# A two-block decode attention kernel on one Trainium2 core: transposing K as fp32 pairs, five of eight heads on VectorE in place of four, and moving copies to ScalarE

## The chip, the cores and the metric

The kernel runs on one core of one Trainium2 chip. The metric is the device time of one execution in microseconds (us); medians are over several executions. A verdict of "faster" or "slower" means more than 2%.

Words used below: PE is TensorE, DVE is VectorE, ACT is ScalarE, POOL is GpSimd, SP is SyncE, which issues all the DMA transfers here. "Landing" is the moment when a part of a transfer reports to its semaphore.

## The reference

Two independent attention blocks, A and B, each with one query token per sequence, 8 sequences, 32 heads, 4096 cached keys and values per head, head size 128, all in bf16. The outputs are set side by side.

```python
def _A_ref(x, k_cache, v_cache, wq, wo):          # _B_ref is the same
    q = (x @ wq).reshape(B, 1, 32, 128).transpose(0, 2, 1, 3)
    scores = einsum("bhqd,bhkd->bhqk", q, k_cache) * 128 ** -0.5
    p = softmax(scores)
    o = einsum("bhqk,bhkd->bhqd", p, v_cache)
    return o.transpose(0, 2, 1, 3).reshape(B, 1, 32 * 128) @ wo
# out = concatenate([A, B], axis=-1)
```

There are 2 blocks x 32 heads x 8 sequences = 512 pairs of (sequence, head); each needs 1 MB of K and 1 MB of V, read once. That is 1.07 GB of 1.11 GB in all, and the data queue fills 96.9% of the DMA engines' time in the profile below, so the loads are the limit to look at first. What can be tuned is what stands in their way.

## The kernel before

A "group" is one head with its 8 sequences; a "K head" is the 1 MB of K of one sequence and head. There are 64 groups. K has 6 slots in SBUF (`Kb`), V has 8 (`Vb`), each of 1 MB. One queue, on SP, issues every load in program order; a K load waits until the head six places earlier has been released.

```python
DL = cfg.get("DL", 10); NK = cfg.get("NK", 6); NV = cfg.get("NV", 8)
DVB = list(cfg.get("DVB", (1, 3, 5, 7)))          # sequences whose scores VectorE computes
PEB = [b for b in range(NB) if b not in DVB]      # the others go through PE
...
def k_released(m):
    if is_pe(m):
        return (pe_tq, NQ * (e_idx(m) + 1))       # all four quarters transposed
    return (dve_qk, v_idx(m) + 1)                 # VectorE's dot products done
...
w = [k_released(n - NK)] if n >= NK else []
    return sp.dma_start(Kb[:, n % NK, :], Ks[blk][b, h].rearrange("(p j) d -> p (j d)", p=128))
```

The scores of a head on the PE path: 32 transposes of 128x128 into PSUM, four evictions to SBUF by ACT, then 32 matmuls with one column of q.

```python
for jj in range(8):                                # emit_T, one quarter of a head
    j = q * 8 + jj
    ins = pe.transpose(dst[:, jj * 128:(jj + 1) * 128], Kb[:, kslot, j * 128:(j + 1) * 128], ident[:])
```

The scores of a head on the VectorE path: 32 dot products over 128 elements, of one position of K per partition with a copy of q that PE has spread over all partitions. In the trace each is two instructions, the product with its sum (8,192 of them, 284 ns in the mean) and the read of the accumulator (8,192, 80 ns), so a head is 64 VectorE instructions.

```python
for jj in range(8):                                # dqk_item, one quarter of a head
    j = 8 * k + jj
    ins = d.tensor_tensor_reduce(junk[:, j, :], Kb[:, kslot, j * 128:(j + 1) * 128], q_rep[:, par, r, :],
                                 1.0, 0.0, ALU.mult, ALU.add, S2[:, par, r, j:j + 1])
```

The softmax then runs per group (maximum on DVE and POOL, exponentials on ACT), PE multiplies with V ten heads later, and the output projection follows. DVE also copies PSUM results that later steps need (`q_rep`, `Dg_sb`, and some small ones) and clears one PSUM bank per group.

## Time and profile before

The median was 2789.04 us of 5 runs (2785.41 to 2790.54).

| engine | busy, us | share of the span |
|---|---|---|
| data queue on the DMA engines | | 96.9% |
| PE | 2051.4 | 74% |
| DVE | 1941.2 | 70% |
| ACT | 714.4 | 26% |

The page of the kernel before, its parts 1 to 4: the busy time of each engine with its number of instructions; the DMA engines' mean busy share and their rate in 40 equal slices of the span; the DMA queues with packets, MB and share of the 16 engines' time; and the chain of work that ended last, by engine ("SPq" and the like are the parts of an engine that issue its instructions; "issue" is time in which an engine waited for nothing that the profile shows).

```profile
PE 2051.4 (74%) x22304; PEld 1352.4 (49%) x22304; DVE 1941.2 (70%) x16975; ACT 714.4 (26%) x2049; POOL 51.8 (2%) x136
...
DMA  9999999989999899998999989999899998999996
GB/s 390 419 419 414 396 420 419 409 357 407 419 417 400 353 416 419 417 398 347 416 419 416 406 339 420 419 414 403 348 419 420 416 409 345 418 419 412 402 396 265
...
q1 hardware_dynamic: 165056, 1107.43, 96.9%
q8 instruction: 179, 2.93, 0.4%
q14 instruction: 174, 1.42, 0.1%
...
DMA 66%; PE 17%; DVE 13%; SPq 2%; issue 1%; ACT 0%; POOL 0%; DVEq 0%; POOLq 0%; ACTq 0%
```

The loads pace the kernel, and PE and DVE wait for them. But the rate is not the 419 GB/s of the best slices throughout: it dips to about 350 at regular places and averages 397. Two lines are the queues of kind "instruction". They carry the engines' own program, as two runs below show: 4,096 more VectorE instructions take q14 from 174 packets to 205 (e1_waits), 8,192 more PE instructions take q8 from 179 to 211 (e9_pewaits). Beside the data queue they are nothing (2.93 and 1.42 MB, 0.4% and 0.1% of the time).

Groups of instructions of the kernel before (line, engine, operation, out<-in, shapes, count | busy us, mean ns of one | idle time before them and what ended it):

```profile
L373 DVE CUSTOM_DVE_ANT_0 junk<-Kb,q_rep 128x128 bf16<-128x128 bf16 x8192 | 1772.4, 284 | 426.4 <-DMA Kb<-in_B_k_cache_dram 200.8
L214 PE MATMUL ps<-ident,Kb 128*128 128x128 bf16 x8192 | 704.1, 265 | 714.5 <-DMA Kb<-in_B_k_cache_dram 361.4
...
L373 DVE DVE_READ_ACCUMULATOR2_ANT S<- 128x1 f32 x8192 | 655.8, 80 | 0.0
```

Both score paths spend hundreds of us idle in front of K loads. One dip, around the load of the second piece of `wq`, in the windows view of the kernel before (stretch in us; stretch's length, then busy time and count of PE, PE's weight loads, DVE, ACT, POOL; granted clock; DMA share; GB/s):

```profile
610.00:620.00 10.00, 10.00 (x136) 6.66 (x135) 7.48 (x67) 2.05 (x4) 0.00 (x0) 1.00 0.92 361
620.00:630.00 10.00, 7.26 (x82) 5.20 (x80) 8.03 (x69) 2.29 (x4) 0.00 (x0) 0.83 0.19 53
630.00:640.00 10.00, 1.57 (x8) 0.48 (x5) 7.06 (x65) 0.00 (x0) 0.36 (x1) 0.84 1.01 416
```

This looks as if the loads stood still for 8 us because nobody had released a slot. The landing records of the trace tell it otherwise. Each of the 1,096 large transfers leaves 16 landings in the trace, which are read here as one from each of the 16 DMA engines that the page counts; no record names the engine of a landing. Sorted by time, for the transfers around this dip (us from the start of the span):

```
transfer   first landing   last landing   later than the last landing before it
V            608.51          627.12          3.42
K            610.99          629.58          2.46
V            613.48          632.09          2.51
wq (2 MB)    618.82          639.10          7.01
K            632.12          641.60          2.50
```

Fifteen of the 16 landings of this batch were in by 621 us, and no first landing came again until 632 us; the last ones went on without a hole. Over the whole trace, the 15 earlier landings of a K or V transfer come 13 to 15 us before the last one in the mean: one landing alone is late, and the author's reading, which no record shows, is that it is always the same engine's. Nothing shows a pause in the late landings: they follow each other at a median of 2.49 us per 1 MB, with 142 gaps that are longer by more than 0.5 us (over 2.5 us for K and V, 7.0 for `wq`, 0.65 for `wo`), nearly all of them by 0.9 to 1.0 us. Of these 142 gaps, 138 stand beside an 8,192-byte packet of q14.

The built program has 17,797 VectorE instructions. PE's count gives an estimate of the size of one: 22,048 matmuls of two instructions each plus 1,296 others are 45,392 in the built program, and q8 carried 2.93 MB in 179 packets of 16,384 bytes, so 64 to 65 bytes each. By that estimate a packet of 8,192 bytes is 128 instructions (e1_waits added 4,096 and 31 packets, 132 a packet), and VectorE's program is 139 such blocks, close to the number of the gaps. (q14 carries more than that: 174 packets here, 204 against 170 blocks in the changed kernel, 61 against 27 in e5_few below, so some 35 more in each. The built program has 4,002 instructions on ACT, POOL and SP, which would be 31 blocks. About 30 packets of q14 stand beside no gap, so by this count it is VectorE's part of q14 that goes with the gaps, not q14 as such.)

### The profile page before, as it was taken

The numbers are of one execution on the slowest core, as the hardware profiler recorded it, in microseconds if no ns is written. First come the engines' busy times: TensorE is split into PE (matmuls) and PEld (weight loads), VectorE is DVE, ScalarE is ACT, GpSimd is POOL, SyncE is SP. The second block draws the span as 40 slices with busy tenths as digits, with TensorE's granted clock in tenths as the row PEclk, the third lists the DMA queues.
The fourth block names the chain that finished last, engine by engine and source line by source line (L and its number), as shares of the span: only waits on it lengthen the run. The fifth ranks groups of instructions, "written<-read, shape, count | busy, mean of one in ns | idle before, by whom it ended". The sixth has DMA issues, their size and how long they took to land.

```text
span 2787.1 us, 68208 instructions
## 1 busy us (share of the span) xinstructions
PE 2051.4 (74%) x22304; PEld 1352.4 (49%) x22304; DVE 1941.2 (70%) x16975; ACT 714.4 (26%) x2049; POOL 51.8 (2%) x136
## 2 busy tenths in 40 slices
PE   6777777776877767777777676776777777777777
PEld 4444454454554544445445454454544444444444
DVE  7777666776767767676676766767767677577775
ACT  3222222222222222222222222222222222222221
POOL 0000000000000000000000000000000000000000
PEclk8898888988889888988898888988888989798889
DMA  9999999989999899998999989999899998999996
GB/s 390 419 419 414 396 420 419 409 357 407 419 417 400 353 416 419 417 398 347 416 419 416 406 339 420 419 414 403 348 419 420 416 409 345 418 419 412 402 396 265
DMA packets 165409, 1111.78 MB, mean 399 GB/s; under 512 B 17569, under 2 KB 17569, under 8 KB 33985
## 3 DMA queue, kind: packets, MB, share of 16 engines
q1 hardware_dynamic: 165056, 1107.43, 96.9%
q8 instruction: 179, 2.93, 0.4%
q14 instruction: 174, 1.42, 0.1%
HBM read 1107.33 MB, written 0.03 MB: 397 GB/s over the span
## 4 chain that ended last, share of the span: by engine, by line
DMA 66%; PE 17%; DVE 13%; SPq 2%; issue 1%; ACT 0%; POOL 0%; DVEq 0%; POOLq 0%; ACTq 0%
DMA Kb<-in_B_k_cache_dram 34%; DMA Kb<-in_A_k_cache_dram 32%; DVE junk L373 12%; PE ps L240 7%; PE ps L214 6%; SPq L629 2%; PE ps L227 1%; PE ps L285 1%; SPq L624 1%; DMA Vb<-in_B_v_cache_dram 1%; DVE S L373 1%; PE ps L263 0%; PE ps L294 0%; DVE acc L417 0%; DVE Dg_sb L578 0%
## 5 line engine op out<-in xcount | busy, mean ns | idle before, releaser
L373 DVE CUSTOM_DVE_ANT_0 junk<-Kb,q_rep 128x128 bf16<-128x128 bf16 x8192 | 1772.4, 284 | 426.4 <-DMA Kb<-in_B_k_cache_dram 200.8
L214 PE MATMUL ps<-ident,Kb 128*128 128x128 bf16 x8192 | 704.1, 265 | 714.5 <-DMA Kb<-in_B_k_cache_dram 361.4
L330 ACT COPY KT<-ps 128x512 f32<-128x512 f32 x1024 | 564.2, 592 | 2019.6 <-PE ps L214 2017.3
L240 PE MATMUL ps<-Vb,Ppad 128*32 128x512 bf16 x4096 | 1038.4, 399 | 3.4 <-issue 1.8
L214 PEld LDWEIGHTS ps<-ident,Kb 128*128 128x128 bf16 x8192 | 651.0, 122 | 791.8 <-DMA Kb<-in_B_k_cache_dram 400.7
L373 DVE DVE_READ_ACCUMULATOR2_ANT S<- 128x1 f32 x8192 | 655.8, 80 | 0.0
L240 PEld LDWEIGHTS ps<-Vb,Ppad 128*32 128x32 bf16 x4096 | 370.4, 100 | 459.3 <-issue 106.9
L227 PEld LDWEIGHTS ps<-q_all,KT 128*128 128x128 bf16 x8192 | 222.8, 96 | 82.4 <-issue 80.2
L227 PE MATMUL ps<-q_all,KT 128*128 128x1 bf16 x8192 | 244.9, 164 | 0.4
L404 DVE TENSOR_TENSOR oT<-ps,rL 128x8 bf16<-128x8 f32 x64 | 10.7, 167 | 242.1 <-PE ps L285 242.1
L349 ACT ACTIVATE Ppad<-S,negM 128x32 bf16<-128x32 f32 x256 | 82.0, 320 | 0.0
L349 ACT ACTIVATE Ppad<-ps,negM 128x32 bf16<-128x32 f32 x256 | 72.9, 285 | 29.9 <-DVE negM L567 29.9
L285 PEld LDWEIGHTS ps<-Sel,Dg_sb 32*128 32x128 f32 x512 | 62.6, 188 | 28.4 <-issue 27.1
L285 PE MATMUL ps<-Sel,Dg_sb 32*128 32x8 f32 x512 | 68.2, 255 | 3.6 <-DVE q_all L385 2.9
L604 POOL PARTITION_ALL_REDUCE M_sb<-m_sb x64 | 23.4, 366 | 2440.2 <-DVE m_sb L537 2440.2
L417 DVE TENSOR_TENSOR acc<-ps,acc 128x64 f32<-128x64 f32 x62 | 13.9, 225 | 69.3 <-PE ps L294 69.0
L349 ACT ACTIVATION_READ_ACCUMULATOR Ppad<-ps,negM 128x1 f32 x256 | 52.0, 203 | 0.0
L578 DVE COPY Dg_sb<-ps 32x512 f32<-32x512 f32 x64 | 43.1, 674 | 12.3 <-PE ps L240 12.3
L349 ACT ACTIVATION_READ_ACCUMULATOR Ppad<-S,negM 128x1 f32 x256 | 51.2, 200 | 0.0
L395 DVE CAST q_rep<-ps 128x512 bf16<-128x512 f32 x64 | 43.7, 682 | 6.5 <-PE ps L274 5.0
L544 DVE MEMSET ps<- 32x512 f32 x64 | 31.0, 485 | 5.9
L567 DVE TENSOR_SCALAR negM<-M_sb 128x8 f32<-128x8 f32 x64 | 11.0, 172 | 31.5 <-POOL M_sb L604 31.5
(29 smaller groups left out, 196.3 us busy)
## 6 DMA issues: line engine op xcount, KB each, us to landing
Kb<-in_A_k_cache_dram SPq DMA_DIRECT2D x256, 1024.0 KB, 25.1
Vb<-in_A_v_cache_dram SPq DMA_DIRECT2D x256, 1024.0 KB, 26.5
Kb<-in_B_k_cache_dram SPq DMA_DIRECT2D x256, 1024.0 KB, 25.4
Vb<-in_B_v_cache_dram SPq DMA_DIRECT2D x256, 1024.0 KB, 26.5
wq_sb<-in_A_wq_dram SPq DMA_DIRECT2D x4, 2048.0 KB, 31.3
wo_sb<-in_A_wo_dram SPq DMA_DIRECT2D x32, 256.0 KB, 26.5
wq_sb<-in_B_wq_dram SPq DMA_DIRECT2D x4, 2048.0 KB, 32.7
wo_sb<-in_B_wo_dram SPq DMA_DIRECT2D x32, 256.0 KB, 26.7
```

The costliest lines, as they stand in the source:

```text
L214: ins = pe.transpose(dst[:, jj * 128:(jj + 1) * 128], Kb[:, kslot, j * 128:(j + 1) * 128], ident[:])
L227: ins = pe.matmul(S[:, c:c + 1], lhsT=KT[:, e_idx(n) % 2, j * 128:(j + 1) * 128], rhs=q_all[:, G, b:b + 1], start=True, stop=True)
L240: ins = pe.matmul(Dg(par), lhsT=Ppad[:, par, b, c].rearrange("p a m -> p (a m)"), rhs=Vb[:, vslot, c * 512:(c + 1) * 512], start=False, st ...
L285: ins = pe.matmul(Mp_f[:, 0:NB], lhsT=Dg_sb[0:32, par, jj * 128:(jj + 1) * 128], rhs=Sel[0:32, jj, :], start=(jj == 0), stop=(jj == 3))
L330: return a.copy(dst, src)
L349: return a.activation(Ppad[:, par, b, :, b, :], src.rearrange("p (c m) -> p c m", m=4), ACTF.Exp, bias=negM[:, par, b:b + 1], scale=SCALE, ...
L373: ins = d.tensor_tensor_reduce(junk[:, j, :], Kb[:, kslot, j * 128:(j + 1) * 128], q_rep[:, par, r, :], 1.0, 0.0, ALU.mult, ALU.add, S2[:, ...
L395: return d.tensor_copy(q_rep[:, G % 2, :, :].rearrange("p r d -> p (r d)"), Mp_f[:, 0:NDV * 128])
L544: return d.memset(Dg(G % 2), 0.0)
L578: return d.tensor_copy(Dg_sb[:, G % 2, :], Dg(G % 2))
L624: return sp.dma_start(Kb[:, n % NK, :], Ks[blk][b, h].rearrange("(p j) d -> p (j d)", p=128))
L629: return sp.dma_start(Vb[:, n % NV, :], Vs[blk][b, h].rearrange("(p j) d -> p (j d)", p=128))
```

## The change

The intent: relieve PE, ACT and the copies, and use VectorE's 30% of free time. K is read as fp32 elements, each a pair of bf16 values, so a head needs 16 transposes in place of 32; the matmuls then take every second column of the result with a q vector that has been permuted and masked (`Qe`). Five of eight sequences go to VectorE in place of four. The copies of `q_rep`, `q_all`, `xT`, `Dg_sb` and `o_sb` go from VectorE to ACT, and the clearing of the PSUM bank is replaced by the start flag of the first matmul. Cut to its core:

```diff
-    DVB = list(cfg.get("DVB", (1, 3, 5, 7)))
+    DVB = list(cfg.get("DVB", (1, 2, 4, 5, 7)))
...
+                if T1:
+                    dst = ktp_f(bank)
+                    kf = Kb[:, kslot, :].bitcast(f32)
+                    for tt in range(4):
+                        t = q * 4 + tt
+                        ins = pe.transpose(dst[:, tt * 128:(tt + 1) * 128], kf[:, t * 128:(t + 1) * 128], ident_f[:])
+                    return ins
...
+                    for tt in range(4):
+                        t = q * 4 + tt
+                        c = b * NJ + 2 * t
+                        for e in range(2):
+                            ins = pe.matmul(S[:, c:c + 2], lhsT=ktb[:, t * 256 + e:(t + 1) * 256:2],
+                                            rhs=Qe[:, G % 2, pe_rank[b], e, :], start=(e == 0), stop=(e == 1))
...
-                                    start=False, stop=(c == NCH - 1), skip_group_check=True)
+                                    start=(b == 0 and c == 0), stop=(b == NB - 1 and c == NCH - 1), skip_group_check=True)
...
+        COPY_ENG = cfg.get("COPY_ENG", "act")
+        def cp(eng, dst, src):
+            return eng.copy(dst, src) if COPY_ENG == "act" else eng.tensor_copy(dst, src)
...
-                    add("dve", f"QSC{s}", w, [(dve_mp, 1)], f)
+                    add(which, f"QSC{s}", w, [(dve_mp, 1)], f)
...
-                return d.memset(Dg(G % 2), 0.0)
-            add("dve", f"ZERO{G}", w, [(dve_z, 1)], f)
```

(Left out: the set-up of the permutation and mask tiles, the small matmul pair per group that makes `Qe`, and the reordering of the maxima.)

## The prediction

> **What bounds the kernel now.** The page's slices show the 16 DMA engines 90% busy or more nearly throughout; the queue table gives the data queue 96.9%, the chain of waits gives DMA 66%. PE is busy 74%, VectorE 70%: no compute engine is the limit.
>
> More exactly, I think one DMA engine is. Every transfer leaves 16 landing records in the trace. From about 30 us on, 15 of them come together and one comes some 13 us later. The last landings follow each other without a hole: median 2.49 us per 1 MB K or V head, except for 142 gaps longer by about 0.97 us (138 us in all). Of those, 138 fall beside an 8192-byte packet of the instruction queue q14 (174 on the page). 8192 bytes would be 128 instructions: the 17,797 VectorE instructions of the built program make 139 such blocks. So my reading: the DMA engine that fetches VectorE's instructions loses about 1 us per fetch and is the slowest. The other 15 wait for it through the K and V slots (the stretch 620 to 630 us at 53 GB/s is such a wait). It never runs dry: the next transfer was issued a median of 28 us, never under 8.7 us after the start, before it finished the last.
>
> [...]
>
> **What the change does.**
> - PE: 16 transposes per K head for 32, 3 of 8 K heads for 4. Matmuls in the program fall from 22,048 to 15,072. PE waits about 710 us for K before (waits view): off the critical path.
> - ACT: loses a quarter of its evictions (564 us before), gains copies (about 0.68 us each). Off the path.
> - VectorE: loses two copies and a memset per group (43.7 + 43.1 + 31.0 us), gains 64 heads of 32 dot products at 0.2125 us (start to start in the timeline), 6.8 us each: +435 us. Busy goes from 1941 to about 2265 us, some 80%. Its waits for PE and PoolE (about 400 us before) still fit; two neighbouring VectorE heads lag the arrivals by some 3 us, inside the 28 us of slack.
> - VectorE instructions: 17,797 to 21,760, so 139 to 170 fetches: +31 at about 0.97 us on the slowest DMA engine.
> - HBM bytes are unchanged.
>
> **Sum.** Nothing removed is on the critical path; about 30 us of DMA work is added to it: 2789 + 30 = 2819 us, range 2806 to 2834. Faster by over 2%: 0.03; within 2%: 0.90; slower by over 2%: 0.07.
>
> **What would show it.** q14 packets up by about 30, q8 packets down; about 172 gaps of 1 us in the last landings; still exactly one late landing of 16; median spacing 2.49 us; VectorE busy 2200 to 2330 us; PE busy well down; mean about 395 GB/s; DMA still over 95% busy and leading the chain.
>
> **What would make it wrong.** Waits between VectorE, ACT and PE (ACT's copies stand in line behind evictions and exponentials) could exceed the slack, so that VectorE paces: over 2845 us. Or the fetches are a coincidence and the time stays at 2789; or PE's fetches, which fall, cost the slowest engine too, and the time falls by tens of us. The end could grow by a few us, two of the last three heads being VectorE's.

## The result, and the profile after

The changed kernel took 2827.93 us (median of 8 runs, 2823.57 to 2829.9) against 2789.87 us of before (15 runs). The ratio is 1.013, 95% interval 1.0115 to 1.0145: slower by 1.3%, within the 2% band. A ratio here is the mean time of one kernel's fast runs over that of the other's in the same rounds, so it is not quite the ratio of the medians.

The page of the changed kernel, the same parts:

```profile
PE 1916.8 (68%) x15328; PEld 1227.2 (43%) x15328; DVE 2272.4 (80%) x20935; ACT 685.6 (24%) x1997; POOL 52.1 (2%) x138
...
DMA  8999999999999899998999989999899998999996
GB/s 357 420 419 418 377 419 418 391 371 389 420 402 395 362 397 419 405 400 348 417 415 407 397 338 420 419 405 399 334 419 416 401 394 344 420 418 398 402 386 260
...
q1 hardware_dynamic: 165056, 1107.43, 96.4%
q8 instruction: 124, 2.03, 0.3%
q14 instruction: 204, 1.67, 0.1%
...
DMA 52%; DVE 31%; PE 13%; SPq 2%; issue 1%; ACT 0%; DVEq 0%; POOL 0%; POOLq 0%
```

The data queue moved the same 1107.43 MB. q14 went from 174 packets to 204, q8 from 179 to 124. PE lost 135 us of busy time, VectorE gained 331. Groups of the changed kernel:

```profile
L409 DVE CUSTOM_DVE_ANT_0 junk<-Kb,q_rep 128x128 bf16<-128x128 bf16 x10240 | 2212.0, 288 | 322.4 <-DMA Kb<-in_B_k_cache_dram 154.7
...
L229 PE MATMUL ps<-ident_f,Kb 128*128 128x128 f32 x3072 | 620.7, 386 | 505.1 <-DMA Kb<-in_B_k_cache_dram 267.0
...
L409 DVE DVE_READ_ACCUMULATOR2_ANT S<- 128x1 f32 x10240 | 849.9, 83 | 0.1
```

Both paths still wait for K loads for hundreds of us, so neither paces the kernel, although VectorE is 80% busy. The dip of the same `wq` load, in the windows view of the changed kernel:

```profile
620.00:630.00 10.00, 9.98 (x77) 6.49 (x78) 6.49 (x62) 2.35 (x4) 0.00 (x0) 0.74 0.97 382
630.00:640.00 10.00, 4.46 (x25) 3.50 (x23) 9.83 (x93) 2.03 (x4) 0.00 (x0) 0.77 0.13 40
640.00:650.00 10.00, 6.13 (x53) 2.96 (x51) 8.22 (x75) 1.17 (x2) 0.37 (x1) 0.84 0.95 364
```

The dip has only moved. The landing records of both profiled runs, counted the same way, and how many us later than in the run before a given transfer had landed (in the order of their last landings, numbered from 0):

```
                                     before   changed
gaps longer by more than 0.5 us         142       170
of these beside a q14 packet            138       164
median spacing of last landings, us    2.49      2.49
last landing of transfer 40, us      114.09    119.41  (+5.3)
last landing of transfer 400, us    1025.16   1041.80  (+16.6)
last landing of transfer 1095, us   2779.01   2815.85  (+36.8)
end of the span, us                  2787.1    2824.4  (+37.3)
```

The waits view has new entries (engine and line, what it waited for: us in total, times, longest us). Before:

```profile
DVE oT L404 <- PE ps L285: 242.1, 64, 5.9
...
DVE acc L417 <- PE ps L294: 69.0, 59, 2.8
```

In the changed kernel:

```profile
PE ps L312 <- DVE Qe L453: 326.3, 64, 18.2
...
DVE acc L476 <- PE ps L332: 158.3, 62, 3.9
...
DVE oT L463 <- PE ps L323: 14.0, 2, 13.2
```

PE now waits for VectorE once per group, and VectorE for PE at another place. Whether such waits matter is decided by the loads: about 5 us are lost in the first 40 us, and the rest comes evenly along the run, as 28 further gaps of 1 us would. A run below tells it too: with the VectorE heads in another order (e8_order), PE's wait for `Qe` is 54 us, and DVE's two waits are back near those of the kernel before (`acc` 64 us, `oT` 244 us), and the time stays that of the changed kernel.

### The profile page after: what moved, and what is told of

It is laid out like the page before. It is cut to its first block, busy times and chain, and to the rows that moved or that the text cites. A ratio compares the mean times of both kernels' runs of the same rounds, so it can differ in the third digit from the quotient of the medians.

```text
span 2824.4 us, 58099 instructions
## 1 busy us (share of the span) xinstructions
PE 1916.8 (68%) x15328; PEld 1227.2 (43%) x15328; DVE 2272.4 (80%) x20935; ACT 685.6 (24%) x1997; POOL 52.1 (2%) x138
## 3 DMA queue, kind: packets, MB, share of 16 engines
q1 hardware_dynamic: 165056, 1107.43, 96.4%
## 4 chain that ended last, share of the span: by engine, by line
DMA 52%; DVE 31%; PE 13%; SPq 2%; issue 1%; ACT 0%; DVEq 0%; POOL 0%; POOLq 0%
DVE junk L409 29%; DMA Kb<-in_B_k_cache_dram 27%; DMA Kb<-in_A_k_cache_dram 24%; PE ps L229 7%; PE ps L269 5%; DVE S L409 1%; SPq L715 1%; SPq L720 1%; DMA Vb<-in_B_v_cache_dram 1%; PE ps L332 1%; DVE Qe L453 0%; PE ps L312 0%; DVE acc L476 0%; PE ps L250 0%; ACT q_rep L417 0%
## 5 line engine op out<-in xcount | busy, mean ns | idle before, releaser
L409 DVE CUSTOM_DVE_ANT_0 junk<-Kb,q_rep 128x128 bf16<-128x128 bf16 x10240 | 2212.0, 288 | 322.4 <-DMA Kb<-in_B_k_cache_dram 154.7
L229 PE MATMUL ps<-ident_f,Kb 128*128 128x128 f32 x3072 | 620.7, 386 | 505.1 <-DMA Kb<-in_B_k_cache_dram 267.0
L409 DVE DVE_READ_ACCUMULATOR2_ANT S<- 128x1 f32 x10240 | 849.9, 83 | 0.1
L229 PEld LDWEIGHTS ps<-ident_f,Kb 128*128 128x128 f32 x3072 | 554.7, 205 | 546.1 <-DMA Kb<-in_B_k_cache_dram 285.4
L366 ACT COPY KT<-ps 128x512 f32<-128x512 f32 x768 | 436.5, 590 | 1188.2 <-PE ps L229 1187.2
L312 PE MATMUL ps<-ident,q_all 128*128 128x128 bf16 x320 | 54.4, 293 | 375.4 <-DVE Qe L453 326.3
L417 ACT CAST q_rep<-ps 128x512 bf16<-128x512 f32 (+1 forms) x128 | 54.5, 426 | 782.9 <-PE ps L312 782.9
L250 PEld LDWEIGHTS ps<-Qe,KT 128*128 128x128 bf16 x6144 | 167.6, 97 | 54.3 <-issue 53.5
L250 PE MATMUL ps<-Qe,KT 128*128 128x2 bf16 x6144 | 182.7, 163 | 0.3
L476 DVE TENSOR_TENSOR acc<-ps,acc 128x64 f32<-128x64 f32 x62 | 13.9, 225 | 158.3 <-PE ps L332 158.3
L586 ACT COPY Dg_sb<-ps 32x512 f32<-32x512 f32 x64 | 36.8, 575 | 103.9 <-PE ps L269 103.9
```

Of the source, the lines that this page charges most:

```text
L229: ins = pe.transpose(dst[:, tt * 128:(tt + 1) * 128], kf[:, t * 128:(t + 1) * 128], ident_f[:])
L250: ins = pe.matmul(S[:, c:c + 2], lhsT=ktb[:, t * 256 + e:(t + 1) * 256:2], rhs=Qe[:, G % 2, pe_rank[b], e, :], start=(e == 0), stop=(e == 1))
L312: ins = pe.matmul(Mp_f[:, r * 128:(r + 1) * 128], lhsT=q_all[:, G, b:b + 1].broadcast_to([128, 128]), rhs=ident[:], start=True, stop=True)
L366: return a.copy(dst, src)
L417: return eng.copy(dst, src) if COPY_ENG == "act" else eng.tensor_copy(dst, src)
L586: return a.copy(Dg_sb[:, G % 2, :], Dg(G % 2))
```

## The experiments

Every run gave correct results. "Blocks" are VectorE instructions of the built program over 128; "gaps" are counted as above, in the profiled run.

| run | VectorE instructions (blocks) | q14 | q8 | VectorE busy, us | gaps | median, us | ratio to before (95%) |
|---|---|---|---|---|---|---|---|
| before | 17,797 (139) | 174 | 179 | 1941 | 142 | 2789 | |
| changed | 21,760 (170) | 204 | 124 | 2272 | 170 | 2828 | 1.013 (1.0115 to 1.0145) |
| e1_waits | 21,893 (171) | 205 | 179 | 1949 | 171 | 2824.1 | 1.0115 (1.0093 to 1.0136) |
| e2_busy | 18,053 (141) | 175 | 179 | 2389 | 142 | 2797.3 | 1.0021 (1.0002 to 1.0039) |
| e3_pairs | 17,600 (138) | 174 | 148 | 1842 | 138 | 2786.7 | 0.9985 (0.9964 to 1.0006) |
| e4_rebal | 22,024 (172) | 202 | 147 | 2365 | 178 | 2835.5 | 1.0158 (1.0136 to 1.018) |
| e5_few | 3,461 (27) | 61 | 179 | 2057 | 29 | 2688.5 | 0.9645 (0.9628 to 0.9663) |
| e6_few_pairs | 3,264 (26) | 62 | 148 | 1958 | 22 | 2682.9 | 0.9621 (0.9607 to 0.9635) |
| e7_few_after | 3,840 (30) | 64 | 124 | 2421 | 31 | 2687.6 | 0.9636 (0.962 to 0.9653) |
| e8_order | 21,760 (170) | 204 | 124 | 2283 | 169 | 2825.7 | 1.0133 (1.0118 to 1.0148) |
| e9_pewaits | 17,797 (139) | 173 | 211 | 1945 | 138 | 2791.1 | 1.0007 (0.9991 to 1.0023) |
| e10_after | 21,760 (170) | 204 | 124 | 2272 | 169 | 2824.8 | 1.013 (1.0116 to 1.0145) |
| e11_order | 21,760 (170) | 204 | 124 | 2282 | 172 | 2825.4 | 1.0133 (1.012 to 1.0146) |
| e12_best | 2,560 (20) | 54 | 124 | 2282 | 23 | 2684.9 | 0.9631 (0.9615 to 0.9647) |

(For e3_pairs and e4_rebal the expectations below have 17,539 and 21,890 instructions; these are the numbers of the programs as built.)

The theory on trial, the author's reading of the 142 gaps and the q14 packets beside them: one DMA engine serves VectorE's instruction fetches, loses about 1 us of loading per fetch, and is the slowest; the kernel's time is that engine's time. What the runs can show of it is landings, packets and time, not the engine. The rivals: VectorE's work itself slows the loads or the releases; the copies on ACT or the pairs make new waits; the rate of the memory is simply a ceiling.

### Instructions without work: e1_waits

The kernel before, with waits on a semaphore that has long been up. In the built program its 8,192 waits are 4,096 instructions more (17,797 to 21,893).

```diff
             def f(d, par=par, r=r, kslot=kslot, k=k):
                 ins = None
+                for _ in range(8):
+                    d.wait_ge(s_id, 1)
```

> The kernel before with 4,096 more VectorE instructions that do nothing: waits on a semaphore that is already up (17,797 to 21,893 instructions, 139 to 171 blocks of 128). VectorE's work is unchanged. Fetch theory: 32 more fetches at about 0.97 us each, +31 us, 2820 us (2813 to 2828), about 30 more q14 packets and about 174 gaps of 1 us. Rival (the change costs VectorE work, or waits between engines): VectorE's busy time is unchanged and so is the time, 2785 to 2795 us.

Measured: ratio 1.0115, which on 2789 us is +32 us (26 to 38). The page of e1_waits, parts 1 and 3:

```profile
PE 2069.0 (73%) x22304; PEld 1360.8 (48%) x22304; DVE 1949.4 (69%) x16975; ACT 716.5 (25%) x2049; POOL 52.1 (2%) x136
...
q8 instruction: 179, 2.93, 0.4%
q14 instruction: 205, 1.68, 0.1%
```

VectorE did the same 16,975 counted instructions for about the same busy time; the added ones do no work and are not even counted as busy. Only q14 grew, by 31 packets, and the gaps grew by 29. Nearly the whole loss of the change came back with nothing but instructions to fetch.

### Work without instructions: e2_busy

One reduction more per VectorE head, into a tile that nobody reads.

```diff
+                if k == 0:
+                    d.tensor_reduce(extra[:], Kb[:, kslot, 0:1664], AX.X, ALU.max)
```

> The kernel before with one extra VectorE reduction over 1,664 elements of each of its 256 K heads: about 1.7 us each, +435 us of VectorE work, as much as the change adds, but only 256 more instructions (2 blocks). Fetch theory: +2 us, plus up to 3 us at the start, 2788 to 2797 us. Rival (VectorE's work or its SBUF reads slow the loads): about +37 us as in the change, 2820 to 2830 us.

Measured: ratio 1.0021, +6 us (1 to 11). The median of 2797.28 us is just over the top of what was expected. The page of e2_busy:

```profile
PE 2059.4 (74%) x22304; PEld 1352.7 (48%) x22304; DVE 2388.9 (85%) x17231; ACT 716.3 (26%) x2049; POOL 50.8 (2%) x136
...
q14 instruction: 175, 1.43, 0.1%
```

VectorE was busier (85%) than in the changed kernel (80%), and the loss was a sixth of the change's. So VectorE's work is not the main cause; but some us do come with it. The two added blocks would make about 2 (an estimate, from 0.97 us a gap), though the gaps of the trace did not grow. In the trace 3 us of it are at the end: from the last landing to the end of the span it takes 11.3 us, 8.1 before.

### The change in parts: e3_pairs and e4_rebal

e3_pairs is the changed kernel with the old split:

```diff
-    DVB = list(cfg.get("DVB", (1, 2, 4, 5, 7)))
+    DVB = list(cfg.get("DVB", (1, 3, 5, 7)))
```

> The changed kernel with the split put back to four heads each; K transposed in pairs and the copies on ACT stay. VectorE has 17,539 instructions (137 blocks against 139), PE 18,080 matmuls against 22,048. Fetch theory: -2 us, 2783 to 2792 us, q14 packets within 5 of before. Rival (the copies on ACT or the pair set-up cause the loss by waits): most of the +37 us stays. Second rival (fewer PE fetches help): clearly under 2780 us.

Measured: 2786.65 us, ratio 0.9985 (0.9964 to 1.0006), the same time as before. Its page, parts 1 and 3:

```profile
PE 2065.3 (74%) x18336; PEld 1337.2 (48%) x18336; DVE 1841.7 (66%) x16839; ACT 791.8 (28%) x2189; POOL 52.4 (2%) x138
...
q8 instruction: 148, 2.42, 0.4%
q14 instruction: 174, 1.43, 0.1%
```

Pairs, copies on ACT and the missing memset neither cost nor gain anything that shows: they work on engines that wait (PE 648 us and VectorE 490 us for K loads in the waits view of this run, ACT 1492 us for PE's transposes).

e4_rebal is the changed kernel with the new split, but without pairs and without the copies on ACT (the start flag in place of the memset stays):

```diff
-    T1 = cfg.get("T1", True)
+    T1 = cfg.get("T1", False)
-        COPY_ENG = cfg.get("COPY_ENG", "act")
+        COPY_ENG = cfg.get("COPY_ENG", "dve")
```

> The changed kernel with the split of five VectorE heads kept, but K transposed in bf16 as before and the copies on VectorE. VectorE has 21,890 instructions (171 blocks, 32 more than before). Fetch theory: +31 us, and about +5 us at the start as in the changed kernel: 2818 to 2834 us. Rival (pairs or copies cause the loss): back near 2789 us.

Measured: 2835.54 us, ratio 1.0158 (1.0136 to 1.018). The loss is all in the rebalance, and it is a little over the top of the range. Its trace has 178 gaps and was already 8 us behind before at transfer 40. With the copies back on it VectorE is 83% busy. The other two parts of the change may hide a part of what the rebalance costs (1.0158 against 1.013), but the two intervals overlap.

### Fewer instructions for the same heads: e5_few, e6_few_pairs, e7_few_after

If fetches are the price, 64 instructions per head are the fault and not the head. The head's quarter becomes one multiplication of 1,024 elements and one sum over it:

```diff
-                for jj in range(8):
-                    j = 8 * k + jj
-                    ins = d.tensor_tensor_reduce(junk[:, j, :], Kb[:, kslot, j * 128:(j + 1) * 128], q_rep[:, par, r, :],
-                                                 1.0, 0.0, ALU.mult, ALU.add, S2[:, par, r, j:j + 1])
+                js = slice(8 * k, 8 * k + 8)
+                d.tensor_tensor(junk[:, js, :], Kb[:, kslot, 1024 * k:1024 * (k + 1)].rearrange("p (j d) -> p j d", d=128),
+                                q_rep[:, par, r, :].unsqueeze(1).broadcast_to([128, 8, 128]), ALU.mult).then_inc(dve_tt, 1)
+                d.wait_ge(dve_tt, 4 * vi + k + 1)
+                ins = d.tensor_reduce(S2[:, par, r, js], junk[:, js, :], AX.X, ALU.add)
```

(The products are now rounded to bf16 before they are summed.)

> The kernel before with VectorE's 64 instructions per K head (32 dot products, each with a read of its accumulator) replaced by 8: four multiplications of 1,024 elements and four sums. VectorE's instructions fall from 17,797 to 3,461, 139 blocks to 27, for the same head count. Fetch theory: 112 fetches fewer on the slowest DMA engine, so that engine's own need falls to about 2789 - 112 x 0.97 = 2680 us; PE's 179 fetches on q8 then show whether another engine is next (estimate: at most 0.77 us each, or that engine would have been the slowest already, so at most 2790). So 2675 to 2765 us, clearly faster, if VectorE keeps pace; by an estimate from the 128-wide reductions a head takes 7 to 9.5 us, 31 to 41 us of a 42 us group, so VectorE may become the limit. Rival (the DMA rate of about 399 GB/s is a ceiling of memory, fetches do not matter): 2785 to 2795 us.

Measured: 2688.48 us, ratio 0.9645. The page of e5_few, parts 1, 2, 3 and 5:

```profile
PE 2012.1 (75%) x22304; PEld 1318.0 (49%) x22304; DVE 2057.1 (76%) x2639; ACT 714.4 (27%) x2049; POOL 53.8 (2%) x136
...
DMA  9999999999999999999999999999999999999996
GB/s 388 420 420 420 417 420 420 420 418 416 420 420 420 405 417 419 420 420 396 419 420 420 420 403 396 419 420 420 396 420 420 420 420 396 421 420 420 420 420 279
...
q1 hardware_dynamic: 165056, 1107.43, 99.4%
q8 instruction: 179, 2.93, 0.4%
q14 instruction: 61, 0.50, 0.0%
...
L376 DVE TENSOR_REDUCE S<-junk 128x8 f32<-128x1024 bf16 x1024 | 1249.4, 1220 | 35.4
```

VectorE is busier than before (2057 against 1941 us), and the kernel is 3.6% faster. The dips are nearly gone: the slices stand at 420 GB/s, the data queue fills 99.4%. So the dips were in the main not the cost of the `wq` load or of slots released too late by the arithmetic; they went with VectorE's instructions (139 blocks to 27, 142 gaps to 29). That 15 engines waited there for the sixteenth is the author's reading. (The 14th, 19th, 24th, 29th and 34th slices, 339 to 353 GB/s before, still read 396 to 405.) 29 gaps are left, most of them by 1.2 to 1.7 us and about 120 us apart; 26 of them stand beside a q8 packet, 5 beside one of q14. PE's fetches come every 15 us (2688 over 179), so a gap is at every eighth.

e6_few_pairs is the same loop in the changed kernel with the old split.

> The same 8 instructions per VectorE head, on the changed kernel's code with the split of four and four: pair transposes, copies on ACT. PE matmuls 18,080 against 22,048, so about 148 fetches on q8 for 179; VectorE 3,264 instructions (26 blocks). Fetch theory: if PE's fetch engine is the next slowest, this run is faster than the one with 179 (31 fetches at the cost that that run shows, up to 20 us); if PE's fetches are free, the two agree within 5 us. Rival: no difference to before.

Measured: 2682.93 us, ratio 0.9621. It is 5.5 us below e5_few in the median, at the edge of what the expectation set apart, with 22 gaps in place of 29, now about 143 us apart: PE's fetches come every 18 us there (2683 over 148), so it is the eighth again. The intervals of the two ratios just overlap.

e7_few_after is the same loop in the changed kernel, five heads on VectorE.

> The changed kernel (five VectorE heads, pairs, copies on ACT) with 8 VectorE instructions per head: 3,840 instructions (30 blocks) for 21,760, q8 about 124 fetches. Fetch theory: the whole loss of the change disappears and more, 2665 to 2750 us, if five heads fit in VectorE's 42 us per group (7 us a head or less); if a head takes over 8.4 us VectorE paces at 5 heads, 2800 us or more, with VectorE over 95% busy. Rival (the change loses because of VectorE's share of the heads): at least 2815 us even with VectorE below 90%.

Measured: 2687.62 us, ratio 0.9636, with VectorE 90% busy. Its page, parts 1 and 3:

```profile
PE 1878.6 (70%) x15328; PEld 1198.7 (45%) x15328; DVE 2421.3 (90%) x3015; ACT 679.8 (25%) x1997; POOL 54.6 (2%) x138
...
q14 instruction: 64, 0.52, 0.0%
```

The rival that blames VectorE's share of the heads needed 2815 us. With few instructions the split makes no difference that shows. Of this run's 31 gaps, 27 stand beside q14 packets again: VectorE's 30 blocks are more than an eighth of PE's 124 packets (15.5); that this is why was not shown.

### Whose fetches: e9_pewaits

The kernel before with 8,192 empty instructions on PE, twice the bytes of e1_waits.

```diff
             def f(pe):
                 dst = ktp_bf(bank)
                 ins = None
+                for _ in range(16):
+                    pe.wait_ge(s_id, 1)
```

> The kernel before with 8,192 more PE instructions that do nothing (waits on a semaphore already up): 32 more 16 KiB blocks on q8, 512 KiB more of fetched instructions, twice the bytes that the 4,096 VectorE waits added on q14. Theory (only fetches that land on the slowest DMA engine cost[...]): no change, 2785 to 2793 us. Rival (any instruction fetch takes its time from the loads): +31 us or more, 2820 us.

Measured: 2791.11 us, ratio 1.0007 (0.9991 to 1.0023): no change. Part 3 of its page:

```profile
q8 instruction: 211, 3.46, 0.5%
q14 instruction: 173, 1.42, 0.1%
```

32 more packets of 16,384 bytes cost nothing, where 31 of 8,192 bytes on q14 had cost 32 us. So it is not the bytes fetched. That it is the DMA engine on which they fall is the author's reading (the gaps at every eighth of PE's fetches fit it too) and was not shown; the runs differ in the fetching engine and in the size of the packets as well, and no record names the DMA engine.

### The start: e8_order, e10_after, e11_order

The changed kernel is 5 us late already at transfer 10. The ninth K load needs head 2's slot, and head 2 is a second VectorE head in a row at a time when VectorE has just begun. So the order of the VectorE heads was changed, not their number:

```diff
-    DVB = list(cfg.get("DVB", (1, 2, 4, 5, 7)))
+    DVB = list(cfg.get("DVB", (1, 3, 5, 6, 7)))
```

> The changed kernel with the five VectorE heads at 1, 3, 5, 6, 7 in place of 1, 2, 4, 5, 7: the number of instructions is the same, but head 2, which holds up the ninth K load at the start, is PE's. Theory (30 us from fetches, 5 us from the start): 2820 to 2825 us, and the tenth to fortieth transfer within 1.5 us of before in place of 5 us late. Rival (the 7 us over the prediction are not from the start): 2825 to 2830 us as the changed kernel.

Measured: 2825.68 us, ratio 1.0133. In the trace the delay at the start went as expected (transfer 40 was +0.1 us from before, in place of +5.3), but the time did not follow. So it was run again beside an unchanged copy.

> The changed kernel once more, unchanged, for its ratio to before in the same rounds as the next run: 1.013, 2824 to 2830 us.

> The changed kernel with the VectorE heads at 1, 3, 5, 6, 7 once more, beside the changed kernel. If the 5 us of the start that its trace no longer shows are gone from the time as well: 2820 to 2824 us, 4 to 6 us under the changed kernel of the same rounds. If they are given back later: within 2 us of it.

Measured: 2824.8 us for the changed kernel and 2825.4 us for the reordered one, ratios 1.013 and 1.0133. The reordered one was +1.3 us at transfer 40, and +37.5 us at the end. The 5 us of the start are real in the trace but removing them does not shorten the run by an amount that these rounds can see; of the two outcomes that e11_order set apart, the second came: the 5 us are given back. A part of that can be seen. With 5, 6 and 7 on VectorE the last three heads of the run are all its own, and from the last landing to the end of the span it takes 13.9 us (e8_order) and 11.1 us (e11_order), against 8.6 us in both profiles of the changed kernel: 5.3 and 2.5 us lost at the end.

### The floor: e12_best

Five heads in the new order, pairs, copies on ACT, and halves in place of quarters, so 4 instructions per head.

```diff
+                if k in (0, 2):
+                    ... d.tensor_tensor(junk[:, js, :], <2,048 elements of K>, <q_rep 16 times>, ALU.mult).then_inc(dve_tt, 1)
+                else:
+                    ... d.wait_ge(dve_tt, 2 * vi + h + 1); d.tensor_reduce(S2[:, par, r, js], junk[:, js, :], AX.X, ALU.add)
```

> Five VectorE heads at 1, 3, 5, 6, 7, pair transposes, copies on ACT, and 4 VectorE instructions per head (two multiplications and two sums of 2,048 elements): 2,560 VectorE instructions, 20 blocks, about 124 fetches on q8. Fetch theory: 2651 us (before, without its 138 us of gaps) plus 20 x 0.97, or 124/8 x 1.5, whichever engine is the slower, about 23 us: 2672 to 2682 us. If VectorE (about 90% busy) falls behind with three heads in a row, 2690 us or more.

Measured: 2684.89 us (2680.85 to 2692.45), 3 us over the top of the range and within the noise of e6_few_pairs. Of its 23 gaps 21 stand beside q8 packets and none beside q14; the data queue reads 100.0%. By that figure the next limit has been reached: the loads themselves fill the DMA engines' time. e6_few_pairs and e12_best beat both kernels, by 3.8% and 3.7% against before; the two cannot be told apart.

## Why the prediction was right

The point was 2819 us (2806 to 2834); the changed kernel took 2824.8 to 2827.9 us. Point by point:

- **The bound: one DMA engine, never dry.** Shown for the landings; that one engine is behind them was not shown. The chain still leads with DMA (52%; VectorE's share of it rose from 13% to 31%, but e7_few_after, with VectorE 90% busy, is faster than both kernels), the spacing stayed at 2.49 us, one landing of 16 is late in both (12.8 us after the fifteenth in the mean before, 13.6 us after the change), and after the start the next transfer was still issued about 7 us or more before the last landing of the one before it.
- **PE and ACT off the critical path.** Shown by e3_pairs: a sixth fewer PE fetches (148 q8 packets for 179) and VectorE's copies on ACT, same time. In the changed kernel the copies that were estimated at 0.68 us took ACT 0.586 us (`q_rep`) and 0.575 us (`Dg_sb`) each.
- **VectorE's busy time.** 2265 us predicted, 2272 measured; 0.2125 us per dot product was the right price.
- **VectorE's waits still fit.** They did, though not as described. DVE's wait for PE's output of the group, 242 us before, is 14 us after, because a VectorE head now stands in its place (with that head back on PE, in e8_order, it is 244 us again); its wait for the projection rose from 69 to 158 us, and PE now waits 326 us for VectorE's `Qe`. All of it lies inside the slack: e8_order has neither of the two longer waits, and the same time.
- **Fetches: +31 at 0.97 us.** Shown. The page has +30 packets and the trace +28 gaps; e1_waits alone gives 32 us (26 to 38) for 32 blocks.
- **The sum was 6 to 9 us short.** The term that was mis-sized is in the main the start. The prediction let two neighbouring VectorE heads lag by some 3 us "inside the 28 us of slack", but it found that slack from about 30 us on, and the changed kernel was 5 us late at transfer 10 already. From there to the last landing the two profiles differ by another 27 us in the gaps and 5 us in the ordinary spacings. The end, which it allowed a few us, did not grow (8.1 us from the last landing to the end of the span before, 8.6 after). Two parts of this are open: the 5 us of the ordinary spacings cannot be assigned, since e1_waits, e2_busy, e3_pairs and e9_pewaits show 3 to 8 us of them against the same profile of before; and no run cures the start without lengthening the end, so that the start costs the time its 5 us is an inference.

Two things stay open besides. No record names the DMA engine, so that VectorE's fetches on q14 and the late landings share one engine is inferred from how they go together (138 of 142 gaps) and from e1_waits, e5_few and e9_pewaits. And a fetch's own packet takes 0.33 us in the trace while the last landings fall back by about 1 us; why three times as much, no run tells. (For PE's 16,384-byte packets, which take 1.07 us, the gaps are up to 1.7 us.)

## What to carry to other kernels

When the loads are the limit and their rate is below that of the best slices, look whether all landings of a transfer are late or one: here 15 of 16 were in 13 to 15 us before the last. If one is, count instructions and not only microseconds. Here VectorE, 70% busy with many tiny instructions, cost time by their number alone (e1_waits: 4,096 more that do no work, 31 more packets on q14, 32 us), and fewer, longer instructions that cost it more time made the kernel faster (e5_few: 8 in place of 64 per head, VectorE busy 2057 us for 1941, 99 us gained with 112 fewer blocks). It was not so for PE (e9_pewaits: 32 more packets on q8, no change).
